# Low parts of the first two batches on GpSimd, another room for VectorE, and an emitted order from the third unit

## The chip, the cores and the metric

The kernel runs on one core of one Trainium2 chip. The metric is device time in microseconds. Three timed runs gave 714.94, 715.07 and 715.30 us; the median is 715.07.

## The reference, cut to what matters

Attention over 4 batches, 8 heads, 576 positions and 64 dimensions a head, and behind it a layer of two products with a squared ReLU:

```python
scores = scale * np.matmul(q, k.transpose(0, 1, 3, 2))
psi_rel = np.log1p(np.abs(rel)); psi_i = np.log1p(np.maximum(pos[:, None], 1.0))
h = np.maximum((psi_rel / psi_i)[..., None] @ w1 + b1, 0.0)
scores = scores + (h @ w2).transpose(2, 0, 1)[None]
attn = np.exp(scores - np.max(scores, axis=-1, keepdims=True))
attn = attn / (np.sum(attn, axis=-1, keepdims=True) + 1e-09)
x = np.matmul(attn, v).transpose(0, 2, 1, 3).reshape(B * S, H * D)
r = np.maximum(x @ w_in, 0.0)
out = (r * r) @ w_out
```

## The kernel before, in words

The attention is cut into 80 units, each of one batch, one pair of heads and one block of query rows. Units 0 to 39 are batches 0 and 1, taken block by block so that the bias, which all batches share, can be made on the way; the first eight are the short last block. Units 40 to 79 are batches 2 and 3, taken pair of heads by pair of heads; every fifth one is a short last block.

In a unit TensorE makes the scores (`sp`), VectorE adds the bias and takes the row extremum (the custom operation on `t`, with `negm`), ScalarE takes the exponential (`p`), TensorE transposes `p` (`pp`, and `pa` for the last columns), ScalarE copies the transposes out (`pt`), and TensorE multiplies with `v` (`px`). In a short last block GpSimd copies 64 columns of `p` first. The tile of scores exists once, so the scores of a unit wait until VectorE has taken the unit before.

The bias is made in 72 steps: VectorE compares distances with thresholds (`mask`), TensorE multiplies the mask with the weights (`bb`), ScalarE and VectorE scale the two results (`bt`), and GpSimd adds them into the table `area`. There are three mask buffers. In units 0 to 7 two or three steps belong to a unit.

The order on an engine comes from two places. Units 0 to 7 run with `plain=True`: a scheduler places their instructions. From unit 8 on the order of TensorE, VectorE and ScalarE is that in which the code emits them, and each bias step first emits the next mask and then its own sum.

In units 40 to 79 the second layer is prepared on the side: weights are read, rounded and split into a high and a low half, and for batches 0 and 1 seven tiles `m` of sums or parts of `x` are made, scaled by `xsig` and split likewise. Five of the seven (`m` = 1, 3, 4, 6, 7) are sums of two blocks; `m` = 2 and 5 are single blocks. Each preparation is a job, a list of stages with an engine, a cost and a function. At the end of every unit `fill` starts the stages whose time has come, as long as the unit's room for that engine lasts; a stage on another engine comes at the earliest a unit later. Before, a sum is three stages: GpSimd adds (`sums_x`), ScalarE scales and rounds to half precision (`high_x`), VectorE scales, subtracts and rounds (`low_x`). Two places hold the sums, so a third sum waits until the first has been used. GpSimd has no room of its own and is not limited.

Behind unit 79 the remaining jobs run out, the first products of the second layer (`ha`, `hb`) begin beside them, and from there TensorE does the second layer: products, a sum of products (`c`), square, split (`gh`, `gl`) and the products with `w_out` (`y`).

Of the kernel before, what the change touches and what calls it, by code (L numbers as in the profile page):

```python
# [17 lines left out]
ALU = mybir.AluOpType  # L18
# [4 lines left out]
HP = H // 2  # L23
# [4 lines left out]
AB = 2  # L28
# [49 lines left out]
def attention_then_relu2_mlp(ctx: ExitStack, tc: tile.TileContext, q, k, v, cols, w_in, w_out, psi, xmat, dist, out):  # L78
    nc = tc.nc
    PE, DVE, ACT, POOL, SP = nc.tensor, nc.vector, nc.scalar, nc.gpsimd, nc.sync  # L80
# [64 lines left out]
    NA = len(units)  # L145
# [352 lines left out]
    def scale_x(b, hp, rows_t):  # L498
        times_rows(b, hp, *spread_rows(rows_t))
# [163 lines left out]
    wdst, xsig, alpha_t = {}, {}, {}  # L663
# [72 lines left out]
    def low_in(n, which=(0, 1)):  # L736
# [5 lines left out]
    width = [256] * B + [128]  # L742
    RIGHT = {
        2: ((0, 0), None, None), 5: ((1, 1), None, None), 3: ((0, 1), ALU.subtract, (1, 1)), 4: ((1, 0), ALU.subtract, (0, 0)),
        1: ((0, 0), ALU.add, (1, 1)), 6: ((0, 0), ALU.add, (0, 1)), 7: ((1, 0), ALU.add, (1, 1)),
    }
    ORDER = (2, 3, 4, 5, 1, 6, 7)
    xs_t = {}
# [15 lines left out]
    split_to = [{m: operand(t[:, 512 * (m - 1):512 * m]) for m in range(1, 8)} for t in xs_at]  # L764
# [7 lines left out]
    def sum_of(n, m):  # L772
        return sum_at.get((n, m), sum_at.get(m))

    def sums_x(n, ms):
        for m in ms:
            for cs, op, a, b in halves(n, m):
                if op:
                    POOL.tensor_tensor(out=sum_of(n, m)[:, :, cs], in0=a, in1=b, op=op)

    def high_x(n, ms):
        for m in ms:
            hi = split_to[n % 2][m][0]
            for cs, op, a, b in halves(n, m):
                ACT.activation(out=hi[:, :, cs], in_=sum_of(n, m)[:, :, cs] if op else a, func=AF.Identity, scale=xsig[n])

    def low_x(n, ms):
        w = width[n]
        for m in ms:
            hi, lo = split_to[n % 2][m]  # L790
            for cs, op, a, b in halves(n, m):
                DVE.scalar_tensor_tensor(out=lo[:, :, cs], in0=sum_of(n, m)[:, :, cs] if op else a, scalar=xsig[n], in1=hi[:, :, cs], op0=ALU.mult, op1=ALU.subtract)
            xs_t[n, m] = (hi[:, :, :w], lo[:, :, :w])

    def store_x(n):
        xs_dram[n] = dram.tile([128, 7 * 512], F32, name=f"xs{n}")
        SP.dma_start(out=xs_dram[n], in_=xs_at[n % 2])
# [40 lines left out]
    def step(s, plain=True):  # L838
        loads(s)
        if plain:  # L840
            scores(s)
        else:
            negm, sps = score_products(s, False)
            exps = [reduce(s, n, negm, sp) for n, sp in enumerate(sps)]
        if s and rest:
            tc.keep_in_program_order(rest.pop(0)())
        n, r = divmod(s, AB * HP)

        def turned():
            for dst, src in transposes((s - TL,)):  # L850
                ACT.copy(dst, src)  # L851

        if not plain:
            rows_made(s - TL)
            turned()
            inverted(s - 1)
            if s >= AB * HP * TAIL:
                scan_first(s)
        if n < TAIL:
            if r == 7 and n + 2 < NIC:  # L860
                tc.keep_in_program_order(scale_xc(chunks[n + 2]))
            if plain:
                bias_upto(NJB * n + BO[r])
                if s == AB * HP - 1:
                    mask_upto(done + MB)
            else:

                def then():
                    mask_upto(done + MB + 1)
                    if exps:  # L870
                        exps.pop(0)()

                sum_upto(NJB * n + BO[r], then)
            if r == 1 and n + 2 < NIC:
                load_xc(chunks[n + 2])
        if plain:
            if s >= TL:
                turned()
        else:
            for fn in exps:  # L880
                fn()
        u = s - TL - 1
        if u >= 0:
            for piece in values((u,)):
                keep_values(*piece)
            if u in norm_of:
                b, hp, ic = units[u]
                scale_x(b, hp, norm_of.pop(u))
# [11 lines left out]
        if u in norm_of:  # L900
            norm_of[u] = norm_copy(norm_rows(norm_of[u]))

    for s in range(AB * HP):
        step(s)
    with tc.manual_schedule(engines={PE.engine, DVE.engine, ACT.engine}):
        for s in range(AB * HP, NA):
            step(s, False)

    scan_stack.close()
# [10 lines left out]
    room = {}  # L920
# [95 lines left out]
    def x_scaled(n, ps_col):  # L1016
        scale_of(n, ps_col)
        if n == 0:
            place_x = raw_tile("w2")
            free = [place_x[:, 512 * k:512 * k + 512] for k in range(2)]  # L1020
            for k, ms in enumerate(((3, 1, 7), (4, 6), (2, 5))):
                stages = []
                for m in ms:
                    if RIGHT[m][1]:
                        sum_at[m] = free[k].rearrange("p (c t) -> p c t", c=2)
                        stages.append(("POOL", 1.3, lambda m=m: sums_x(0, (m,))))
                    stages.append(("ACT", 0.71, lambda m=m: high_x(0, (m,))))
                    stages.append(("DVE", 0.74, lambda m=m: low_x(0, (m,))))
                jobs.insert(len(norms), [max(now[0], first[groups[AB * HP + AB]] + 1), stages])
        else:  # L1030
            free = [a.rearrange("p (c t) -> p c t", c=2) for a in (take(1, 4480, 512), take(0, 9856, 512))]
            for k, ms in enumerate(((3, 1, 7), (4, 6), (2, 5))):
                stages = []
                for m in ms:
                    if RIGHT[m][1]:
                        sum_at[n, m] = free[k]
                        stages.append(("POOL", 1.3, lambda m=m: sums_x(n, (m,))))
                    stages.append(("ACT", 0.71, lambda m=m: high_x(n, (m,))))
                    stages.append(("DVE", 0.74, lambda m=m: low_x(n, (m,))))
                job(dest_at[-1] + 1, *stages)  # L1040

    dest_at = [50] + [60] * 6 + [70]
# [49 lines left out]
    sum_at = {}  # L1092
    with tc.manual_schedule():
        job(NA + 1, *(("DVE", 0.68, lambda k=k: scan(k)) for k in range(SCANS, NF)))
        x_job(NA + 4, 0)
        x_job(NA + 7, 1)
        for u in range(NA - TL - 1, NA):
            norm_job(u)
        for s in range(NA, NU + TL + 3):
            now[0] = s  # L1100
            full = s < NU and units[s][2] < TAIL
            room["DVE"] = min(room.get("DVE", 0), 0.3) + (1.65 if full else 2.5)
            room["ACT"] = min(room.get("ACT", 0) + (0.55 if full else 1.9), 0.6 if full else 1.5)
            loads(s)
            if s == NA:
                for tag, name in zip("dbac", ("pa", "pp", "pp", "px")):
                    held[tag] = bank(name, tag)
                for m, tag in enumerate(raws[:NF - SCANS]):
                    fetch_in(ins[SCANS + m], tag)
            if s < NU:  # L1110
                negm, sps = score_products(s, False)
            fill(s, 3)
            px_now[0] = None
            us = [u for u in ((s - 3, s - 2) if s % 2 else (s - 2, s - 1)) if u < NU]
            pieces = []
            sms = [lambda n=n: softmax(s, n, negm, sps[n]) for n in range(len(sps))] if s < NU else []
            if s % 2 == 0:
                if s == NA and NA - 3 in pt_t:
                    for piece in values((NA - 3,), "c"):
                        keep_values(*piece)  # L1120
                for m, c in enumerate(transposes(us, iter("bacb" if s == NA else "abca")) if us else ()):
                    ACT.copy(*c)  # L1122
            else:
                pieces = values(us, "d") if us else []
            fill(s, 0)
            for fn in sms:
                fn()
            if s < NU and ends(s):
                norm_job(s)
            kept = 0  # L1130
            if any(j[0] <= s and j[1][0][0] == "LAST" for j in jobs):
                kept = max(room["DVE"] - 0.6, 0)
                room["DVE"] -= kept
            fill(s, 1)
            fill(s, 2)
            for piece in pieces:
                keep_values(*piece)
            if kept:
                room["DVE"] += kept
                fill(s, 1)  # L1140
# [31 lines left out]
    sum_at = {3: xT[0][:, 0:2, 128:384], 4: xT[0][:, 2:4, 128:384], 1: take(0, 9856, 512).rearrange("p (c t) -> p c t", c=2)}  # L1172
# [121 lines left out]
    with tc.manual_schedule():  # L1294
# [3 lines left out]
        for i in range(NI + 1):  # L1298
# [4 lines left out]
            n, P = items[min(i, NI - 1)]  # L1303
# [102 lines left out]
```

## Time and profile before

| | |
|---|---|
| median of three runs | 715.07 us |
| profiled execution | 715.1 us |
| its span, first to last instruction | 713.3 us |
| TensorE busy | 685.8 us, 96% |
| VectorE busy | 552.0 us, 77% |
| ScalarE busy | 474.6 us, 67% |
| GpSimd busy | 196.3 us, 28% |
| granted TensorE clock, mean | 0.992 |

The busy share is a mean over stages. Here 1165 instructions of VectorE lie mostly in the first half of the span, in which the attention runs; the second layer leaves VectorE room. A wait of TensorE in the first half moves all that comes behind it.

### The profile page before, as it was taken

To read this page: it belongs to the slowest core of one execution; us is meant where nothing else is said; L and a number is where in the kernel's file an instruction comes from. 1 tells how busy PE (TensorE), PEld (TensorE's weight loads), DVE (VectorE), ACT (ScalarE), POOL (GpSimd) and SP (SyncE) were. 2 spreads that over 40 slices of the span, in tenths; PEclk is the share of its full clock that TensorE was granted. 3 is DMA by queue.
4 is the path that set the end of the run, shared out by engine and by line. 5 is a ranking of instruction groups with operands and counts; after the bars stand their busy time and mean duration, and the time that the engine had idled before them with its cause. 6 is when DMAs were issued, how large, how long until landed. Compare 5 with 4: busy or idle time off the path is not lost.

```text
span 713.3 us, 17398 instructions
## 1 busy us (share of the span) xinstructions
PE 685.8 (96%) x6966; PEld 566.9 (79%) x6966; DVE 552.0 (77%) x1165; ACT 474.6 (67%) x954; POOL 196.3 (28%) x313
## 2 busy tenths in 40 slices
PE   7899999999999999999999999999999999999992
PEld 6568888887787877778788888888888888888881
DVE  8998888876788998998888868687567974566761
ACT  5678878878777999997666757765575554464220
POOL 6564544442111344653223113121111220000000
PEclk9999999999999999999999999999999999999996
DMA  6740000007476134101901433230076403433100
GB/s 190 195 131 3 19 2 3 2 12 230 168 243 208 55 88 131 67 31 51 364 1 61 174 137 119 78 144 1 1 251 250 148 19 145 174 107 119 60 2 29
DMA packets 31620, 75.13 MB, mean 105 GB/s; under 512 B 5556, under 2 KB 13876, under 8 KB 30516
## 3 DMA queue, kind: packets, MB, share of 16 engines
q1 hardware_dynamic: 31540, 74.03, 30.8%
q8 instruction: 55, 0.90, 0.5%
q14 instruction: 25, 0.20, 0.1%
HBM read 55.66 MB, written 18.35 MB: 104 GB/s over the span
## 4 chain that ended last, share of the span: by engine, by line
PE 84%; DVE 8%; ACT 3%; issue 2%; POOL 1%; DMA 0%; SPq 0%; ACTq 0%; DVEq 0%; POOLq 0%
PE y L1283 28%; PE ha L1191 13%; PE px L547 10%; PE sp L425 10%; PE hb L1191 9%; PE pp L529 8%; PE bb L383 4%; DVE t L438 2%; DVE mask L373 2%; ACT pt L1122 1%; PE pa L521 1%; DVE bt L391 1%; ACT p L445 1%; DVE xT L496 0%; PE ra L490 0%
## 5 line engine op out<-in xcount | busy, mean ns | idle before, releaser
L1191 PEld LDWEIGHTS <-area 128*128 128x128 f16 x1680 | 147.7, 98 | 25.3 <-issue 8.7
L1283 PE MATMUL y<-w,gh 128*128 128x512 f32 x576 | 149.0, 398 | 0.6 <-ACT gh L1227 0.6
L1283 PEld LDWEIGHTS y<-w,gh 128*128 128x128 f32 x576 | 105.1, 188 | 22.3 <-ACT gh L1227 1.3
L438 DVE CUSTOM_DVE_ANT_0 t<-sp,area 128x576 f32<-128x576 f32 x144 | 104.2, 754 | 23.0 <-PE sp L425 12.4
L445 ACT ACTIVATE p<-t,negm 128x576 f32<-128x576 f32 x144 | 113.3, 798 | 2.6 <-DVE negm L438 2.0
L425 PE MATMUL sp<-k,q 64*128 64x288 f32 (+1 forms) x640 | 98.8, 426 | 3.3 <-DVE negm L438 1.7
L547 PE MATMUL px<-pt,v 128*64 128x128 f32 (+1 forms) x1600 | 92.2, 266 | 0.9 <-DVE bt L391 0.7
L547 PEld LDWEIGHTS px<-pt,v 128*64 128x64 f32 x1600 | 79.2, 137 | 13.5 <-ACT pt L1122 6.4
L1191 PE MATMUL ha<-area 128*128 128x256 f16 (+1 forms) x816 | 85.1, 260 | 0.7 <-DVE c L1208 0.7
L399 POOL TENSOR_TENSOR area<-bt,bt 128x256 f32<-128x256 f32 x72 | 64.8, 907 | 66.1 <-DVE bt L391 65.9
L1283 PE MATMUL y<-w,gl 128*128 128x512 f32 x288 | 79.0, 390 | 0.0
L529 PE MATMUL pp<-ident,p 128*128 128x128 f32 x576 | 77.6, 277 | 0.9 <-DVE bt L391 0.8
L529 PEld LDWEIGHTS pp<-ident,p 128*128 128x128 f32 x576 | 62.4, 141 | 15.5 <-ACT p L445 6.6
L425 PEld LDWEIGHTS sp<-k,q 64*128 64x128 f32 (+1 forms) x640 | 52.8, 175 | 23.5 <-issue 6.5
L1191 PE MATMUL hb<-area 128*128 128x256 f16 (+1 forms) x612 | 64.7, 260 | 0.0
L1283 PEld LDWEIGHTS y<-w,gl 128*128 128x128 f32 x288 | 54.1, 188 | 12.2 <-DVE gl L1228 0.2
L373 DVE TENSOR_TENSOR mask<-sdist,theta 128x1024 f16<-128x1024 f16 x81 | 58.1, 727 | 2.8 <-PE bb L383 0.6
L851 ACT COPY pt<-pp 128x512 f32<-128x512 f32 x68 | 36.9, 589 | 25.4 <-PE pp L529 25.4
L383 PE MATMUL bb<-wmov,mask 128*128 128x64 f16 x1296 | 46.7, 195 | 5.0 <-DVE mask L373 4.8
L383 PEld LDWEIGHTS <-mask 128*128 128x128 f16 x1296 | 43.8, 100 | 9.3 <-DVE mask L373 7.4
L1122 ACT COPY pt<-pp 128x512 f32<-128x512 f32 x76 | 41.5, 605 | 13.3 <-PE pp L529 13.0
L1228 DVE TENSOR_TENSOR gl<-area,gh 128x512 fp32r<-128x512 f32 (+1 forms) x40 | 25.3, 668 | 27.4 <-ACT gh L1227 25.6
(161 smaller groups left out, 993.0 us busy)
## 6 DMA issues: line engine op xcount, KB each, us to landing
raw<-in_w_in SPq DMA_DIRECT2D x32, 512.0 KB, 3.9
r<-in_w_out SPq DMA_DIRECT2D x16, 512.0 KB, 5.1
xs<-area SPq DMA_DIRECT2D x4, 1792.0 KB, 12.7
py<-o SPq DMA_DIRECT2D x12, 512.0 KB, 3.0
o<-py SPq DMA_DIRECT2D x12, 512.0 KB, 4.5
v<-in_v SPq DMA_DIRECT2D x16, 320.0 KB, 4.1
q<-in_q SPq DMA_DIRECT2D x32, 128.0 KB, 3.3
out<-o SPq DMA_DIRECT2D x8, 512.0 KB, 2.9
```

The source lines that it names most:

```text
L373: DVE.tensor_tensor(out=out, in0=win, in1=th, op=ALU.is_ge)
L383: PE.matmul(bb[:, 64 * (7 - r):64 * (8 - r)], lhsT=m[:, r], rhs=wmov[:, n], start=(n == 0), stop=(n == 1))
L399: POOL.tensor_tensor(out=dst, in0=tw, in1=sw, op=ALU.add)
L425: mm = PE.matmul(out_t[to, x, :HALF], lhsT=qt[rows, cols], rhs=kt[rows, k0:k0 + HALF], start=True, stop=True)
L438: DVE.tensor_tensor_reduce(out=t.rearrange("p (x n) -> p x n", x=2), in0=sp[:, :, :HALF], in1=bias.rearrange("p (x n) -> p x n", x=2), sca ...
L445: ACT.activation(out=p[:, S * n:S * n + S], in_=t, func=AF.Exp, bias=negm[:, n:n + 1], scale=-1.0, accum_out=sums[:, 2 * ic + n:2 * ic + n ...
L529: PE.transpose(pp[:, 128 * c:128 * c + 128], p[:, k0:k0 + 128], ident)
L547: PE.matmul(px[64 * h:64 * h + 64, 128 * m:128 * m + w], lhsT=vt[:, c, h], rhs=src, start=(c == 0), stop=(c == 4))
L851: ACT.copy(dst, src)
L1122: ACT.copy(*c)
L1191: PE.matmul(h[:, s, :w], lhsT=a, rhs=x, start=(k == 0), stop=(k == 5))
L1283: PE.matmul(y_t[n][k], lhsT=(gl if m == 2 else gh)[:, slot, o:o + 128], rhs=wl if m == 1 else wh, start=((n, P) in firsts and f == 0 and m ...
```

## The change

There are three edits. First, units from 2 on, not from 8 on, use the emitted order (`FREE = 2`). Second, for batches 0 and 1 the five sums have other stages: GpSimd adds and multiplies by the scale in place, ScalarE copies the result to half precision, GpSimd subtracts; the two single blocks keep their stages. Third, VectorE's room for a full unit is 1.6 in even and 1.35 in odd units instead of 1.65, and GpSimd gets a room of 3.2 a unit.

```diff
+    def scaled_sum(n, m):
+        sums_x(n, (m,))
+        t = sum_of(n, m)[:, :, :width[n]]
+        POOL.tensor_scalar(out=t, in0=t, scalar1=xsig[n], scalar2=None, op0=ALU.mult)
+
+    def high_sum(n, m):
+        w = width[n]
+        ACT.copy(split_to[n % 2][m][0][:, :, :w], sum_of(n, m)[:, :, :w])
+
+    def low_sum(n, m):
+        w = width[n]
+        hi, lo = (x[:, :, :w] for x in split_to[n % 2][m])
+        POOL.tensor_tensor(out=lo, in0=sum_of(n, m)[:, :, :w], in1=hi, op=ALU.subtract)
+        xs_t[n, m] = (hi, lo)
+
+    def split_stages(n, m, free):
+        if not RIGHT[m][1]:
+            return [("ACT", 0.71, lambda: high_x(n, (m,))), ("DVE", 0.74, lambda: low_x(n, (m,)))]
+        sum_at[n, m] = free
+        return [("POOL", 2.5, lambda: scaled_sum(n, m)), ("ACT", 0.62, lambda: high_sum(n, m)), ("POOL", 1.3, lambda: low_sum(n, m))]
...
-                if s == AB * HP - 1:
+                if s == FREE - 1:
                     mask_upto(done + MB)
...
-    for s in range(AB * HP):
+    FREE = 2
+    for s in range(FREE):
         step(s)
     with tc.manual_schedule(engines={PE.engine, DVE.engine, ACT.engine}):
-        for s in range(AB * HP, NA):
+        for s in range(FREE, NA):
             step(s, False)
...
-                    if RIGHT[m][1]:
-                        sum_at[n, m] = free[k]
-                        stages.append(("POOL", 1.3, lambda m=m: sums_x(n, (m,))))
-                    stages.append(("ACT", 0.71, lambda m=m: high_x(n, (m,))))
-                    stages.append(("DVE", 0.74, lambda m=m: low_x(n, (m,))))
+                    stages += split_stages(n, m, free[k] if k < 2 else None)
...
-            room["DVE"] = min(room.get("DVE", 0), 0.3) + (1.65 if full else 2.5)
+            room["DVE"] = min(room.get("DVE", 0), 0.3) + ((1.6, 1.35)[s % 2] if full else 2.5)
+            room["POOL"] = min(room.get("POOL", 0), 0) + 3.2
```

On VectorE, in units 6 and 7 (`L438` is the bias and extremum of a unit's scores, `L373` a mask, `L391` the scaled result of a bias step), there stood before:

```order
L438 ISA t,negm<-sp,area 128x576
L438 ISA negm 128x1
L373 TENSOR_TENSOR mask<-sdist,theta 128x1024 x3
L391 TENSOR_TENSOR bt_1027<-bb,xc 128x256
L391 TENSOR_TENSOR bt_1051<-bb,xc 128x256
L391 TENSOR_TENSOR bt_1075<-bb,xc 128x256
L438 ISA t,negm<-sp,area 128x576
```

and now there stands:

```order
L438 ISA t,negm<-sp,area 128x576
L438 ISA negm 128x1
L373 TENSOR_TENSOR mask<-sdist,theta 128x1024
L391 TENSOR_TENSOR bt_1039<-bb,xc 128x256
L373 TENSOR_TENSOR mask<-sdist,theta 128x1024
L391 TENSOR_TENSOR bt_1065<-bb,xc 128x256
L373 TENSOR_TENSOR mask<-sdist,theta 128x1024
L391 TENSOR_TENSOR bt_1089<-bb,xc 128x256
L438 ISA t,negm<-sp,area 128x576
```

The instructions are the same; masks and results of bias steps now alternate.

On GpSimd, around units 55 to 59 of the second attention stage (`L779` adds two blocks, `L720` to `L722` are the sums of a weight tile, `L447` the copy of a short block's `p`), there stood before:

```order
L467 CAST parts<-sums 128x9
L779 TENSOR_TENSOR raw<-xT_82 128x512
L720 TENSOR_TENSOR raw<-wa 128x256
L721 TENSOR_TENSOR raw<-wa 128x256
L722 TENSOR_TENSOR raw<-wa 128x128
L779 TENSOR_TENSOR raw<-xT_82 128x512
L447 COPY p<-p 128x64
```

and now there stands (`L798` is the multiplication, `L807` the subtraction, `L734` the high part of a weight tile):

```order
L467 CAST parts<-sums 128x9
L807 TENSOR_TENSOR area<-raw,area 128x512
L779 TENSOR_TENSOR raw<-xT_82 128x512
L798 TENSOR_SCALAR raw<-raw,small 128x512
L720 TENSOR_TENSOR raw<-wa 128x256
L721 TENSOR_TENSOR raw<-wa 128x256
L722 TENSOR_TENSOR raw<-wa 128x128
L807 TENSOR_TENSOR area<-raw,area 128x512
L734 TENSOR_SCALAR area<-wa,small 128x256
L807 TENSOR_TENSOR area<-raw,area 128x512
L779 TENSOR_TENSOR raw<-xT_82 128x512
L798 TENSOR_SCALAR raw<-raw,small 128x512
L447 COPY p<-p 128x64
```

Between the same two copies of small tiles and of `p`, GpSimd has six more instructions: two multiplications, three subtractions and the high part that stood later.

On VectorE, in unit 57 (`L792` is a low part, `L200` and `L201` the last steps of a weight tile, `L197` and `L198` its first steps), there stood before:

```order
L438 ISA t,negm<-sp,area 128x576
L438 ISA negm 128x1
L792 SCALAR_TENSOR_TENSOR area<-raw,small,area 128x512
L200 SCALAR_TENSOR_TENSOR wa<-raw,wa 128x512
L201 SCALAR_TENSOR_TENSOR wa<-raw,wa 128x512
L560 COPY xT_3936<-px 128x64
L560 COPY xT_3937<-px 128x128
```

and now there stands:

```order
L438 ISA t,negm<-sp,area 128x576
L438 ISA negm 128x1
L197 TENSOR_SCALAR wa<-wa 128x512
L198 TENSOR_SCALAR wa<-wa 128x512
L560 COPY xT_3936<-px 128x64
L560 COPY xT_3937<-px 128x128
```

The low part has left VectorE, and the weight tile is two steps further back.

## Rows read from the trace of the kernel before

**Rows 1.** Busy time by engine in 20 us (count), granted clock, DMA share, GB/s:

```profile
240.00:260.00 20.00, 19.49 (x222) 15.38 (x224) 19.40 (x48) 18.80 (x46) 10.74 (x17) 1.00 0.21 58
```

**Rows 2.** Waits of TensorE, 0 to 62 us: total, times, longest:

```profile
PE bb L383 <- DVE mask L373: 4.8, 9, 0.9
```

**Rows 3.** Waits of TensorE, 189 to 326 us:

```profile
PE sp L425 <- DVE negm L438: 1.7, 6, 0.4
PE sp L425 <- DVE sums L459: 1.2, 2, 0.6
```

**Rows 4.** Waits of TensorE, 326 to 700 us:

```profile
PE ha L1191 <- DVE c L1208: 0.7, 1, 0.7
PE y L1283 <- ACT gh L1227: 0.6, 1, 0.6
```

**Rows 5.** Busy time of the masks alone, by stretch, with their count:

```profile
24.00:54.00 30.00, 14.77 (x20) 1.00 0.55 152
54.00:100.00 46.00, 15.34 (x23) 1.00 0.03 9
```

**Rows 6.** Timeline of VectorE, 38 to 58 us (start, length, idle before):

```profile
39.00 0.76 DVE L438 CUSTOM_DVE_ANT_0 t<-sp,area 128x576 f32<-128x576 f32 x1 [0.47 <-PE sp L425]
...
57.52 0.76 DVE L438 CUSTOM_DVE_ANT_0 t<-sp,area 128x576 f32<-128x576 f32 x1 [0.96 <-PE sp L425]
```

**Rows 7.** VectorE by form, 230 to 330 us: busy us, mean ns, idle before:

```profile
L201 DVE SCALAR_TENSOR_TENSOR wa<-raw,wa 128x512 uint32<-128x512 uint32 x7 | 4.8, 692 | 0.2
...
L792 DVE SCALAR_TENSOR_TENSOR area<-area,small 128x512 f16<-128x512 f32 x5 | 4.3, 865 | 0.0
...
L792 DVE SCALAR_TENSOR_TENSOR area<-raw,small,area 128x512 f16<-128x512 f32 x5 | 4.1, 818 | 0.0
```

**Rows 8.** GpSimd by form, 190 to 342 us:

```profile
L467 POOL CAST parts<-sums 128x9 bf16<-128x9 f32 x33 | 8.5, 258 | 26.0 <-DVE sums L460 12.8 <-DVE sums L459 11.8
L734 POOL TENSOR_SCALAR area<-wa,small 128x256 f16<-128x256 f32 x8 | 7.9, 988 | 0.0
...
L779 POOL TENSOR_TENSOR raw<-xT 128x512 f32<-128x512 f32 x5 | 6.5, 1306 | 0.8 <-DVE area L792 0.6 <-DMA v<-in_v 0.2
L721 POOL TENSOR_TENSOR raw<-wa 128x256 f32<-128x256 f32 x8 | 6.5, 808 | 0.0
L469 POOL TENSOR_TENSOR sums<-sums,parts 128x9 f32<-128x9 f32 x22 | 6.3, 288 | 1.8
L720 POOL TENSOR_TENSOR raw<-wa 128x256 f32<-128x256 f32 x8 | 6.2, 780 | 16.8 <-ACT p L445 12.7 <-DVE wa L201 4.1
L722 POOL TENSOR_TENSOR raw<-wa 128x128 f32<-128x128 f32 x8 | 4.8, 602 | 0.0
```

**Rows 9.** Timeline of GpSimd at units 54 and 74:

```profile
245.11 0.24 POOL L447 COPY p<-p 128x64 f32<-128x64 f32 x1 [11.55 <-ACT p L445]
...
313.12 0.24 POOL L447 COPY p<-p 128x64 f32<-128x64 f32 x1 [2.31 <-ACT p L445]
```

**Rows 10.** Timeline of ScalarE at units 60 and 77:

```profile
260.61 0.71 ACT L785 ACTIVATE area<-raw,small 128x512 f16<-128x512 f32 x1
262.26 1.57 ACT L1122 COPY pt<-pp 128x512 f32<-128x512 f32 x3 [0.94 <-PE pp L529]
263.70 0.47 ACT L1122 COPY pt<-pa 128x128 f32<-128x128 f32 x2
...
322.12 0.73 ACT L785 ACTIVATE area<-area,small 128x512 f16<-128x512 f32 x1
```

**Rows 11.** Timeline of TensorE, 250 to 266 us, the values of unit 61:

```profile
265.04 1.20 PE L547 MATMUL px<-pt,v 128*64 128x128 f32 x18
```

**Rows 12.** Timeline of VectorE ahead of the second layer:

```profile
333.33 1.79 DVE L201 SCALAR_TENSOR_TENSOR wa<-raw,wa 128x512 uint32<-128x512 uint32 x1
```

**Rows 13.** Timeline of VectorE, one form beside small and large GpSimd operations:

```profile
250.64 0.43 DVE L198 TENSOR_SCALAR wa<-wa 128x512 int32<-128x512 int32 x1
...
257.73 1.39 DVE L198 TENSOR_SCALAR wa<-wa 128x512 int32<-128x512 int32 x1
```

More of the change, by code (lines that the diff above doesn't have):

```diff
@@ L1023, in x_scaled @@
                 for m in ms:
-                    if RIGHT[m][1]:
[L1025 to L1028, printed above, removed]
+                    stages += split_stages(0, m, free[k].rearrange("p (c t) -> p c t", c=2) if k < 2 else None)
                 jobs.insert(len(norms), [max(now[0], first[groups[AB * HP + AB]] + 1), stages])
@@ L1034, in x_scaled @@
                 for m in ms:
-                    if RIGHT[m][1]:
-                        sum_at[n, m] = free[k]
-                        stages.append(("POOL", 1.3, lambda m=m: sums_x(n, (m,))))
-                    stages.append(("ACT", 0.71, lambda m=m: high_x(n, (m,))))
-                    stages.append(("DVE", 0.74, lambda m=m: low_x(n, (m,))))
+                    stages += split_stages(n, m, free[k] if k < 2 else None)
                 job(dest_at[-1] + 1, *stages)
```

## The prediction

> **What bounds the kernel now.** I read the busy times by stretch first, then the waits of TensorE, and then, for the two stages that the change touches, the timelines of VectorE, GpSimd and ScalarE. TensorE is busy almost throughout, and its clock is granted in full in every stretch quoted here, so time can be won only where TensorE waits. In the second attention stage it is busy 19.49 of 20 us beside a VectorE at 19.40 and a ScalarE at 18.80, while GpSimd, at 10.74, has near half its time free [rows 1]. In the first 62 us the largest wait of TensorE is for masks that VectorE makes, 4.8 us in nine waits [rows 2]. From 189 to 326 us it waits 1.7 and 1.2 us for VectorE, in eight waits before score groups [rows 3]. From 326 to 700 us two waits are left, 0.7 and 0.6 us, both where the second layer begins [rows 4]. After that TensorE runs through to the end, and what is won or lost before is carried to the end in full. The profiled execution took 715.1 us (span 713.3 and 1.8 outside it), the median of the three timed runs is 715.07: the sum below is made against 715.1 and needs no correction.
>
> **The change part by part.**
>
> *Emitted order from unit 2.* No instruction is added or removed. Units 2 to 7 stand on VectorE as mask, sum, mask, sum instead of two or three masks and then the sums, and the value product of a unit comes one unit earlier on TensorE. This is how units from 8 on already stand, and there the rows show what it does to a mask: 23 of them take 15.34 us, 0.67 each, where the 20 before 54 us take 14.77, 0.74 each [rows 5]. The difference is 0.07 x 20 = 1.4 us of VectorE, which bounds TensorE here. The long ones are masks that come second or third in a row, while GpSimd adds up the sums of the bias step before. VectorE's own waits in the stretch, such as the 0.47 us before 39.00, could go too; about 1.1 us are idle there. So the bounds are 2.5 us won and, if an emitted unit makes VectorE wait for its scores as the one at 57.52 does for 0.96 us [rows 6], 0.5 lost. I take 1.4 won, the mask term alone.
>
> The Trainium skill, SBUF — State Buffer, section "SBUF: two separate sides", says that VectorE and GpSimd share one pair of ports as an exclusive lock: an operation in a two-port mode or with two SBUF inputs holds off a GpSimd operation that started later, and is held off by one that started earlier, for the whole instruction. The masks agree with it (0.67 against 0.74). It would make the first stage's term what I took, and it speaks against the next part.
>
> *The low parts.* Ten low passes leave VectorE: five at 865 ns and five at 818 ns, 8.4 us together [rows 7]. In exchange the room that the planner gives VectorE falls from 1.65 to 1.6 and 1.35 a unit, so its list gets shorter in some units and stays as long in others. In unit 57 a low pass and the two last steps of a weight tile become two first steps of another, which are shorter; in units 59 and 60 the list stays about as it was. Of the 2.9 us of waits I let 1.0 go; the bounds are 0 and 2.9.
>
> GpSimd gets ten multiplications and ten subtractions. The subtraction has the shape of the sum, 1.31 us. The multiplication is not in the trace; nearest is the one of half the width, 0.99 us [rows 8]. If its length did not matter it would stay 0.99, if all of it grew 1.98. The two-input operation grows from 0.78 to 1.31 over the same step, a factor 1.68, which would make it 1.66. But at half width the multiplication takes longer than the two-input operation although it reads half as much, so a good part of it is a fixed cost; I take 1.3, the middle of 0.99 and 1.66, and keep 0.99 and 1.98 as ends.
>
> The Trainium skill, GPSIMD Engine Reference, section 4.1 "Engine selection", calls one-input operations there "roughly line-rate"; at its 1.2 GHz that would be 0.43 us for 512 columns. Rows 8 do not agree: 256 columns take 0.99.
>
> What matters is who waits. ScalarE's conversion of a sum now stands behind GpSimd's multiplication, and in ScalarE's queue the copies that empty TensorE's transposes stand behind that conversion. For batch 0 GpSimd cannot begin before its copy at 245.11 is done, at 245.35 [rows 9]. From there to the last multiplication it has seven two-input operations (9.17), the parts of one inverse (3 x 0.258 + 2 x 0.288 = 1.35), the sums of a weight tile (0.78 + 0.81 + 0.60 = 2.19), its high part (0.99), and three multiplications (3.9): 17.6 us, end at 262.95. ScalarE reaches that place at 260.61 and begins the copies behind it at 262.26 [rows 10]. Now they begin 0.52 after 262.95, at 263.47, 1.21 late; they ended at 264.17 and were needed by the values at 265.04 [rows 11], so 0.87 is spare: 0.3 us lost. For batch 1 it begins at 313.36 [rows 9] and has four two-input operations, one inverse and two multiplications before the place that ScalarE reaches at 322.12 [rows 10]: 5.24 + 1.35 + 2.6, end at 322.55, 0.4 lost, no spare counted. Together 0.7 lost; with 0.99 for the multiplication nothing, with 1.98 it is 2.4 + 1.8 = 4.2. On ScalarE itself a conversion replaces an activation of the same width: nothing.
>
> *The end of the stage.* GpSimd's low part of the output tile 2 comes one unit earlier. Before, it fell on a VectorE operation that then took 1.79 us, where that form has a mean of 0.69 [rows 7, 12], just ahead of the sums that TensorE waits for (0.7). I take 0.4 of the 1.3 us [rows 4] as won; bounds 1.3 won and 0.7 lost, if the later weight tile comes late from GpSimd.
>
> Sum: -1.4 - 1.0 + 0.7 - 0.4 = -2.1, so 713.0 us.
>
> **The rivals.**
>
> *GpSimd becomes the bound.* The place is unit 59 and unit 77, where ScalarE waits for the multiplication with all its copies behind it. For it: the queue above is full without a gap for 17.6 us, VectorE has some sixteen operations of the locking kind beside it, and one such operation was held 1.39 us instead of 0.43 by a sum of GpSimd [rows 13]. Against it: only half of GpSimd is used now. With 1.98 for the multiplication 4.2 us are lost; if two of the sixteen are held as that one was, 1.9 us, VectorE's gain of 1.0 turns into a loss of 0.9; the end gives nothing. -1.4 + 0.9 + 4.2 = +3.7: 718.8 us. It decides when GpSimd's waits and locks cost more than 4.2 us, 1.4 above the 2.8 that the other parts bring.
>
> *The parts cancel.* With 1.66 for the multiplication GpSimd costs 1.4 + 1.15 = 2.6, the masks give 1.4, VectorE 1.0 and the end nothing: +0.2, 715.3 us. The same comes out if the emitted order does not do what it says, because the scores wait as at 57.52, and the rest stays as forecast less the end: about 714.8.
>
> *GpSimd is never late.* If the multiplication stays under one us, its term is nothing, more of VectorE's waits go (2.2), the masks give 1.8 and the end 1.0: -5.0, 710.1 us. Against it stands the 0.99 at half width.
>
> **How the numbers follow.** The forecast, 711.5 to 713.6, gets 0.42, GpSimd never late 0.10, the parts cancel 0.30, GpSimd the bound (with all between 716.5 and 720) 0.18. A measurement here tells 0.2%, 1.4 us, from no change; so faster 0.52, same 0.30, slower 0.18. The range runs from 710.8, in the case without lateness, to 716.9, part of the way to the slow rival, and leaves about one in ten on each side.
>
> **What would show it.** Unit 10's first score group before 58.4 instead of 59.66, with masks before 54 us at 0.67 to 0.69 on the mean, shows the first term. The multiplication's mean says which case holds: above 1.6 the forecast fails. ScalarE's conversions waiting for GpSimd, in units 57, 59 and 77, show the loss; TensorE's waits for VectorE from 189 to 326 us should fall from 2.9 to about 1.9. The forecast is wrong if TensorE waits for copies or values behind those conversions for more than 3 us in sum, or if VectorE's forms beside GpSimd grow so that its busy time does not fall by at least 5 us.

## The result and the profile after

The changed kernel takes 722.29 us (median of four runs, 722.02 to 722.63) against 715.11 us: ratio 1.0102, interval 1.009 to 1.0114. Of all runs below, one of e1 and one of the kernel before took 1146.87 and 947.99 us at a granted clock of 0.56 and 0.68; they are left out of the ratios. The forecast was 713.0 with a range up to 716.9. It was slower by 7.2 us where a gain of 2.1 was forecast. The rival in which GpSimd becomes the bound had the direction and the places, and gave 718.8.

Where the time went is read from the beginning of units on TensorE (the first score product of each, in the traces of both kernels):

| first score product of | before, us | after, us | after minus before |
|---|---|---|---|
| unit 10 | 59.66 | 58.56 | -1.10 |
| unit 58 | 253.05 | 252.01 | -1.04 |
| unit 59 | 256.64 | 257.16 | +0.52 |
| unit 61 | 263.87 | 264.98 | +1.11 |
| unit 62 | 266.86 | 269.39 | +2.53 |
| unit 72 | 300.48 | 303.08 | +2.60 |
| unit 73 | 304.28 | 307.94 | +3.66 |
| unit 78 | 321.09 | 325.25 | +4.16 |
| unit 79 | 324.39 | 330.15 | +5.76 |
| second layer (`y`) | 342.94 | 350.05 | +7.11 |

So 1.1 us are won in the first stage, 3.6 lost in units 58 to 61, 1.06 in unit 72, 0.5 in 75 to 77, 1.6 in unit 78 and 1.35 ahead of the second layer. (The start of the second layer is that of its first product with `w_out`, `y`.) After that both kernels run alike.

What TensorE waits for from 189 to 333 us in the changed kernel, and then ahead of the second layer (total, times, longest; [rows 3, 4] are those of before):

```profile
PE pp L529 <- ACT rows L479: 3.0, 2, 1.6
PE sp L425 <- DVE negm L438: 2.3, 6, 0.5
PE pa L521 <- POOL p L447: 1.0, 1, 1.0
PE sp L425 <- DVE sums L459: 0.9, 2, 0.6
PE pa L521 <- DVE xT L560: 0.8, 1, 0.8
PE px L547 <- ACT pt L1137: 0.8, 1, 0.8
...
PE ha L1206 <- DVE c L1223: 1.5, 1, 1.5
PE y L1298 <- ACT gh L1242: 0.7, 1, 0.7
PE hb L1206 <- DVE c L1225: 0.3, 1, 0.3
```

The waits for VectorE before score groups were 2.9 and are 3.2: nothing has gone there. New are the waits for ScalarE's rows and copies, for GpSimd's copy of a `p` and for VectorE's `xT`. Behind the first of them stands ScalarE, and behind ScalarE GpSimd. What ScalarE waits for from GpSimd, 240 to 330 us (total, times, longest):

```profile
ACT area L802 <- POOL raw L798: 5.4, 2, 3.4
ACT area L802 <- POOL area L798: 1.9, 1, 1.9
```

GpSimd in the same stage, by form (busy us, mean ns; [rows 8] are those of before):

```profile
L798 POOL TENSOR_SCALAR area<-area,small 128x512 f32<-128x512 f32 x5 | 8.8, 1769 | 0.5
...
L798 POOL TENSOR_SCALAR raw<-raw,small 128x512 f32<-128x512 f32 x5 | 8.4, 1678 | 1.5 <-DVE small L225 1.1
...
L807 POOL TENSOR_TENSOR area<-raw,area 128x512 f16<-128x512 f32 x5 | 5.8, 1164 | 0.0
```

The multiplication takes 1.68 and 1.77 us on the mean, 1.57 where nothing disturbs it; 1.3 had been taken, with 1.98 as the upper end. The subtraction takes 1.16, less than the 1.31 of a sum. The queue of batch 0 in time order, to be read beside [rows 9] (start, length, and in brackets the idle time before with its releaser):

```profile
235.28 1.57 POOL L798 TENSOR_SCALAR raw<-raw,small 128x512 f32<-128x512 f32 x1
243.69 0.24 POOL L447 COPY p<-p 128x64 f32<-128x64 f32 x1 [6.84 <-ACT p L445]
243.89 1.17 POOL L807 TENSOR_TENSOR area<-raw,area 128x512 f16<-128x512 f32 x1
...
253.43 1.62 POOL L798 TENSOR_SCALAR raw<-raw,small 128x512 f32<-128x512 f32 x1
...
262.42 2.06 POOL L798 TENSOR_SCALAR raw<-raw,small 128x512 f32<-128x512 f32 x1
264.43 0.23 POOL L447 COPY p<-p 128x64 f32<-128x64 f32 x1
```

Three things stand here. GpSimd is idle for 6.84 us because the first subtraction is queued behind the copy of a `p` that has to wait for a softmax; ScalarE had the high part ready at 240.0. Then the queue is full: from 243.89 to the end of the last multiplication at 264.48 it runs 20.6 us without a gap. And the next copy of a `p`, at 264.43, is itself behind that multiplication, so TensorE waits directly for GpSimd. ScalarE and TensorE at the two places:

```profile
255.08 0.62 ACT L802 CAST area<-raw 128x512 f16<-128x512 f32 x1 [2.06 <-POOL raw L798]
...
264.51 0.62 ACT L802 CAST area<-raw 128x512 f16<-128x512 f32 x1 [3.37 <-POOL raw L798]
```

```profile
255.92 0.66 PE L529 MATMUL pp<-ident,p 128*128 128x128 f32 x4 [1.62 <-ACT rows L479]
...
264.72 0.33 PE L521 MATMUL pa<-ident,p 128*128 128x128 f32 x1 [1.04 <-POOL p L447]
...
266.98 1.89 PE L547 MATMUL px<-pt,v 128*64 128x128 f32 x40 [0.76 <-ACT pt L1137]
```

VectorE was to have 8.4 us less to do. Its busy time over the whole stage, from the first score product of unit 40 to 6 us past that of unit 79, before and after (second number after the window: TensorE, then weight loads, VectorE, ScalarE, GpSimd, each with its count):

```profile
189.74:330.39 140.65, 137.42 (x1615) 110.40 (x1612) 123.39 (x313) 123.71 (x304) 49.99 (x106) 1.00 0.37 116
```

```profile
188.64:336.15 147.51, 138.44 (x1615) 110.57 (x1612) 121.60 (x306) 122.20 (x304) 79.29 (x126) 1.00 0.36 111
```

VectorE fell by 1.8 us only, while GpSimd rose by 29.3. Three steps of weight tiles came into this stretch from behind it, but that is the smaller part: from unit 40 to the first `y`, VectorE's 333 and 323 instructions differ by the ten low passes and nothing else, and its busy time is 134.2 us before and 133.4 after. So nearly all of the 8.4 went back into operations that became longer. In unit 72, VectorE's list now has two pairs of first steps of a weight tile in a row, beside the sums of a weight tile and of batch 1 on GpSimd:

```profile
302.84 0.55 DVE L197 TENSOR_SCALAR wa<-wa 128x512 f32<-128x512 f32 x1
303.42 0.83 DVE L198 TENSOR_SCALAR wa<-wa 128x512 int32<-128x512 int32 x1
304.18 0.68 DVE L197 TENSOR_SCALAR wa<-wa 128x512 f32<-128x512 f32 x1
304.89 1.38 DVE L198 TENSOR_SCALAR wa<-wa 128x512 int32<-128x512 int32 x1
```

Two pairs are 1.7 us alone (0.42 and 0.43 each); here they are 3.4, and unit 73 begins 1.06 us later.

### The profile page after: what moved, and what is told of

Same layout as the page of the kernel before. It is cut to its first block, busy times and chain, and to the rows that moved or that the text cites. A ratio compares the mean times of both kernels' runs of the same rounds, so it can differ in the third digit from the quotient of the medians.

```text
span 720.3 us, 17411 instructions
## 1 busy us (share of the span) xinstructions
PE 685.8 (95%) x6966; PEld 567.5 (79%) x6966; DVE 551.3 (77%) x1155; ACT 471.9 (66%) x954; POOL 225.9 (31%) x333
## 4 chain that ended last, share of the span: by engine, by line
PE 83%; DVE 6%; POOL 4%; ACT 2%; issue 2%; DMA 1%; SPq 0%; ACTq 0%; POOLq 0%; DVEq 0%
PE y L1298 28%; PE ha L1206 13%; PE sp L425 10%; PE px L547 9%; PE hb L1206 9%; PE pp L529 8%; PE bb L383 4%; DVE mask L373 1%; DVE t L438 1%; ACT pt L1137 1%; POOL area L807 1%; PE pa L521 1%; POOL raw L798 1%; POOL raw L779 1%; DMA raw<-in_w_in 1%
## 5 line engine op out<-in xcount | busy, mean ns | idle before, releaser
L438 DVE CUSTOM_DVE_ANT_0 t<-sp,area 128x576 f32<-128x576 f32 x144 | 104.2, 753 | 28.4 <-ACT p L445 13.1
L373 DVE TENSOR_TENSOR mask<-sdist,theta 128x1024 f16<-128x1024 f16 x81 | 58.0, 720 | 2.5 <-PE bb L383 0.5
L720 POOL TENSOR_TENSOR raw<-wa 128x256 f32<-128x256 f32 x16 | 12.2, 763 | 111.9 <-issue 65.8
```

What stands on the lines that cost most here:

```text
L373: DVE.tensor_tensor(out=out, in0=win, in1=th, op=ALU.is_ge)
L438: DVE.tensor_tensor_reduce(out=t.rearrange("p (x n) -> p x n", x=2), in0=sp[:, :, :HALF], in1=bias.rearrange("p (x n) -> p x n", x=2), sca ...
```

## The experiments

Four theories stood against each other. Theory 1: GpSimd's own work is too long, and ScalarE waits for its multiplications. Theory 2: two-input operations of GpSimd and VectorE's operations hold each other. Theory 3: the low parts stand in GpSimd's queue behind the copy of a `p`. Theory 4: the rooms place VectorE's list badly. Times below are medians of a kernel's runs, ratios are against the kernel before on the same chip. Profiled executions of the same first stage differ by up to 1.3 us there (unit 10 begins at 57.94 in e11 and at 59.28 in e5; the last section tells of the clock behind it), so single places are compared by the length of units.

**e1: the emitted order alone** (`FREE = 2` on the kernel before).

> The kernel before with the emitted order from unit 2 and nothing else. All theories that put the loss behind 240 us say that the 1.1 us won at unit 10 in the changed kernel stay to the end: 714.0. If the gain of the first stage was given back later (a wait that only moved), 715.1.

713.74 us, ratio 0.9984 (0.9975 to 0.9994). The first part of the change is a gain of 1.1 us that stays to the end. All that follows is compared with this kernel; the changed one is 8.6 us above it (8.4 by the ratios, since the two were timed on different chips).

**e2: no multiplication.**

```diff
     def scaled_sum(n, m):
         sums_x(n, (m,))
-        t = sum_of(n, m)[:, :, :width[n]]
-        POOL.tensor_scalar(out=t, in0=t, scalar1=xsig[n], scalar2=None, op0=ALU.mult)
```

> The changed kernel without the ten multiplications on GpSimd; the sums of batches 0 and 1 stay unscaled, so their values are others. Theory 1 (GpSimd's own work is too long, ten times 1.7 us, and ScalarE waits for it): the waits of ScalarE for GpSimd of 2.1, 3.4 and 1.9 us go, and of the 8.3 us lost behind unit 10 at least 5 come back: 716 to 717.5. Theory 2 (GpSimd's two-input operations and VectorE hold each other; a multiplication reads one operand and does not count): 721 to 722. Theory 3 (the first low parts stand in GpSimd's queue behind the copy of a p and start 3.7 us late, the length of the work is secondary): 719 to 720.

718.26 us, ratio 1.005 (1.0037 to 1.0063): 4.0 us come back, less than theory 1 said and more than theories 2 and 3. ScalarE no longer waits for GpSimd at all, yet 4.5 us of the 8.6 are left. One loss has even grown: units 54 to 57 take 1.7 us longer than before, where the changed kernel had 0.4, and TensorE waits 5.2 us for VectorE before score groups. Where GpSimd is not late, its operations meet VectorE's at another place.

**e3: the copy of `p` on ScalarE** (second attention stage only).

```diff
-                POOL.tensor_copy(out=p[:, S:S + 64], in_=p[:, S - 64:S])
+                (ACT.copy if u >= NA else POOL.tensor_copy)(p[:, S:S + 64], p[:, S - 64:S])
```

> The changed kernel with the copy of a short block's p, in the second attention stage, on ScalarE in place of GpSimd; nothing in GpSimd's queue waits for a softmax any more. Theory 3: the first low part starts at 240.0 instead of 243.9, the wait of TensorE for the p copy (1.0) goes too, and 3 to 4 us of batch 0's 3.7 come back, nothing of batch 1's: 718.3 to 719.3. Theory 1: GpSimd is full from 244 to 264 all the same and ScalarE only waits a little less: 721 to 722. Theory 2: 722.

719.48 us, ratio 1.007 (1.0057 to 1.0083): 2.8 us come back with no instruction less. The first subtraction now begins when ScalarE has its high part:

```profile
239.69 1.17 POOL L807 TENSOR_TENSOR area<-raw,area 128x512 f16<-128x512 f32 x1 [3.24 <-ACT area L802]
```

and ScalarE's waits for GpSimd fall from 7.3 to 0.3 us. Theory 3 explains the larger part of batch 0's loss: units 54 to 61 are 1.7 us longer than before instead of 4.0. Units 72 to 78 are 3.3 us longer, in the changed kernel 3.2, although ScalarE's wait of 1.9 there is gone. What remains in this kernel is VectorE's: TensorE waits 6.3 us for it before score groups (2.9 before), the longest 1.7.

**e4: the rooms of before** (VectorE 1.65, no limit for GpSimd).

> The changed kernel with VectorE's room at 1.65 again and no limit on GpSimd's: the planner lets GpSimd begin its work sooner. Theory 4 (the room tables place the work badly): 719 to 720.5. Theories 1 and 2: within 1 us of the changed kernel, 721.3 to 723.3, since no work goes.

725.12 us, ratio 1.0147 (1.0134 to 1.0161). A miss on both sides: ScalarE's waits for the multiplications grow from 7.3 to 10.1 us, and in the profiled execution TensorE's granted clock falls to 0.50 from 252 to 254 us (1.2 GHz, the lower of its two levels), behind four us in which TensorE was busy 2.0. The two new rooms together are not what makes the changed kernel slow. What each of them is worth this run does not show, since it sets back both, and in that execution a part of the 2.8 us is the clock's.

**e5: emitted order and copy of `p` on ScalarE, low parts on VectorE.**

> The kernel before with the emitted order from unit 2 and the copy of p on ScalarE, the low parts still on VectorE. The copy mattered only where GpSimd is full: then nothing is gained beside the emitted order alone, 713.7 (713.3 to 714.1). If the copy by itself helps or hurts (ScalarE gets eight copies of some 0.2 us), 712.7 or 714.7.

714.62 us, ratio 0.9999 (0.999 to 1.0008). Without the low parts on GpSimd the copy gains nothing; it costs some 0.9 us against e1, so the 2.8 of e3 are the queue's. The cost arises by unit 58: GpSimd begins a sum at 243.29 now, no longer behind the copy, and beside its sums VectorE's `L201` at 243.85 takes 1.65 us and its `L198` at 250.87 takes 1.38, where e1 has 0.69 and 0.43. That is theory 2 in a kernel that has no low part on GpSimd.

**e6: a one-input operation in place of the subtraction** (with the copy as in e3).

```diff
-        POOL.tensor_tensor(out=lo, in0=sum_of(n, m)[:, :, :w], in1=hi, op=ALU.subtract)
+        POOL.tensor_scalar(out=lo, in0=hi, scalar1=ones[:, 0:1], scalar2=None, op0=ALU.mult)
```

> The changed kernel with the copy of p on ScalarE, and in place of GpSimd's subtraction (two operands from memory) a multiplication by one of the high part (one operand, same width, same place in the queue); the low parts then hold the high parts. What is left over of the loss beside the copy alone (719.5 against 713.7) is 5.8 us. Theory 2 (locks by two-input operations): ten of twenty two-input operations of GpSimd go, so VectorE's operations of the forms L197, L198, L200, L201 and L792 are held less, and 2 to 4 us come back: 715.5 to 717.5. Theory 1 (length of GpSimd's work): the replacement is no shorter (1.2 to 1.7 instead of 1.16), so 719.5 to 721.

718.58 us, ratio 1.0053 (1.004 to 1.0066), 0.9 under e3: between the two. The replacement took 1.62 us instead of 1.16, so it was no clean test: fewer full holds, but longer work. That one-input operations lengthen VectorE's too is shown by the table under e9.

**e7: copy on ScalarE and no multiplication.**

> The changed kernel with the copy of p on ScalarE and without the ten multiplications (values unscaled). Either alone gave 718.3 (no multiplications) and 719.5 (copy). Theory 2: with ScalarE no longer waiting for GpSimd, the rest is locks by sums and subtractions, which neither edit touches: 717.8 to 718.6, the two don't add up. If the length of GpSimd's work still matters after the waits of ScalarE are gone, they add up: 715.5 to 716.5.

717.75 us, ratio 1.0037 (1.0024 to 1.005). The edits do not add up: both take away ScalarE's wait for GpSimd, which is 0.3 us in e3 already. Still the multiplications' going gives 1.7 us against e3, so they cost by another way too (table under e9). What is left, 4.0 us above e1, is not ScalarE's wait.

**e8 and e10: one batch only.** In e8 batch 1's low parts are on VectorE again, in e10 batch 0's (there with VectorE's room at 1.65).

> The changed kernel with the low parts of batch 1 on VectorE again (batch 0's stay on GpSimd), the rooms as in the changed kernel. Of the 8.6 us between the emitted order alone and the changed kernel, 3.6 arose by unit 62, the rest from unit 72 on: if the two batches are separate stretches, 713.7 + 3.6 = 717.3, with the later part as in the emitted order alone; if batch 1's loss comes from what batch 0's left behind (a planner's backlog, the smaller rooms), 720 to 722.

> The changed kernel with the low parts of batch 0 on VectorE and VectorE's room at 1.65 again; batch 1's stay on GpSimd, GpSimd's room 3.2. Batch 0 alone gave 719.4, 5.7 above the emitted order; both give 8.6. If the batches add up, batch 1 costs 2.9: 716.6. If the queue of GpSimd is short enough with one batch, 714 to 715.

e8: 719.42 us, ratio 1.0064 (1.005 to 1.0079). e10: 717.38 us, ratio 1.0033 (1.0021 to 1.0046). Above e1 that is 5.7 and 3.6, together 9.3 against the 8.6 of the full change: the batches about add up, though the two runs have different rooms. e10 was missed by 0.8 and e8 by 2.1: the 1.06 of unit 72 is in e8 as well, though batch 1 is on VectorE, and it is not in e10. So it hangs on the rooms and not on the low parts.

**e9: no low parts at all** (the ten are set to zero by a memset of 0.53 us on GpSimd; copy of `p` on ScalarE, rooms as changed).

> The changed kernel with the copy of p on ScalarE and no low parts of the ten sums at all: no multiplication, no subtraction, only a memset of the low parts to zero on GpSimd (the values lack the low parts); ScalarE scales as before the change. Planner, rooms and VectorE's list stay as changed. Theory 2 (what is left beside the copy and the multiplication, 717.75 against 713.74, comes of VectorE and GpSimd holding each other): most of the 4.0 goes, 713.5 to 715; the 1.06 at unit 72 stays, since it is sums of a weight tile and of batch 1 that hold VectorE there and they stay. Theory 4 (VectorE's list under the new rooms is late by itself): 717 to 718.

716.05 us, ratio 1.0016 (1.0007 to 1.0025). Of the 5.7 us between e3 and e1, 3.4 hang on what GpSimd does for the low parts. VectorE shows it. From unit 40 to the second layer, e3 and e9 have the same list of VectorE's instructions in the same order. In the stage of the attention they take (the first is e3, VectorE third)

```profile
188.30:333.50 145.20, 137.73 (x1615) 110.66 (x1612) 124.02 (x306) 124.61 (x312) 76.69 (x118) 1.00 0.35 113
```

```profile
188.94:330.20 141.26, 137.64 (x1615) 110.43 (x1612) 118.19 (x306) 124.64 (x312) 51.25 (x108) 1.00 0.36 116
```

so 5.8 us of VectorE's time are there because of what GpSimd does beside it. e6 and e7 have this list too:

| all with the copy on ScalarE | GpSimd's work for the low parts | VectorE busy, 306 instructions, us | time, us |
|---|---|---|---|
| e3 | ten multiplications, ten subtractions | 124.0 | 719.48 |
| e6 | ten multiplications, ten multiplications by one | 122.9 | 718.58 |
| e7 | ten subtractions | 120.5 | 717.75 |
| e9 | ten memsets | 118.2 | 716.05 |

Theory 2 had said that a multiplication, which reads one operand, does not count. It does: the ten of them are 3.5 us of VectorE's time between e3 and e7, the ten subtractions 2.3 between e7 and e9.

But 2.3 us of the loss against e1 stay in e9 although nobody makes low parts any more, and neither theory had that: 1.05 at unit 72, and 1.4 from unit 79 to the second layer, where three waits are 2.4 us together (1.3 in two waits in e1):

```profile
PE ha L1204 <- DVE c L1221: 1.4, 1, 1.4
PE y L1296 <- ACT gh L1240: 0.7, 1, 0.7
PE hb L1204 <- DVE c L1223: 0.3, 1, 0.3
```

**e11: VectorE's room 1.75 and 1.55 by parity, on e1.**

> The emitted order from unit 2 with the low parts on VectorE and its room at 1.75 in even and 1.55 in odd units, in place of 1.65. A candidate: of the 2.9 us of waits for VectorE between 189 and 326 us, 1 may go (712.7) if they come of odd units with too long a list; if the lists are late wherever they stand, 713.2 to 714.7.

713.68 us, ratio 0.9983 (0.9974 to 0.9992): the same as e1. The two are the fastest kernels found; both beat the kernel before and the changed one.

**e12: one tile of ten** (the first of batch 0 on GpSimd, VectorE's room 1.65; GpSimd's room of 3.2 stays, which e1 does not have).

> The emitted order from unit 2, VectorE's room 1.65, and only one of the ten low parts (the first tile of batch 0, where GpSimd stands idle for 7 us) on GpSimd, its multiplication 1.57 and subtraction 1.17. A candidate: VectorE's list is 0.84 shorter in one unit: 713.0 to 713.7 if nothing is held; 714 to 715 if the planner only fills the room with a step that GpSimd holds.

716.29 us, ratio 1.0012 (1.0003 to 1.0021); above both expected ranges. Its runs fall into two groups, near 714.5 at a mean granted clock of 0.993 and near 716.6 at 0.989, with one between. VectorE, then GpSimd, in the profiled execution, which is of the slower group:

```profile
248.61 1.72 DVE L792 SCALAR_TENSOR_TENSOR area<-xT,small,area 128x512 f16<-128x512 f32 x1
250.26 1.50 DVE L197 TENSOR_SCALAR wa<-wa 128x512 f32<-128x512 f32 x1
251.79 0.58 DVE L198 TENSOR_SCALAR wa<-wa 128x512 int32<-128x512 int32 x1
```

```profile
248.63 1.15 POOL L807 TENSOR_TENSOR area<-raw,area 128x512 f16<-128x512 f32 x1
249.87 1.60 POOL L779 TENSOR_TENSOR raw<-xT 128x512 f32<-128x512 f32 x1
```

The low pass of 0.75 is held through the whole subtraction to 250.34, and the next step, 0.42 alone, through the sum to 251.76: 2.05 us, and TensorE's longest wait for scores here is 2.0. This is theory 2 at one place, without any lateness of GpSimd: ScalarE waits for no multiplication in this kernel. The wait has a sequel on TensorE (busy first, granted clock third from the end):

```profile
252.00:254.00 2.00, 0.13 (x2) 0.16 (x4) 2.00 (x6) 0.92 (x3) 0.62 (x1) 1.00 0.00 0
254.00:256.00 2.00, 2.00 (x12) 1.29 (x13) 1.18 (x4) 1.58 (x4) 0.00 (x0) 0.67 0.03 8
256.00:258.00 2.00, 2.00 (x12) 2.00 (x11) 2.00 (x6) 1.17 (x2) 0.27 (x1) 0.50 0.00 0
```

Behind the wait the clock is at the lower of its two levels (1.2 GHz) until about 258, and unit 58 takes 1.33 us longer than in e1. So the 2.6 us against e1 are two things: the faster group is 1.1 above the faster of e1's two groups (near 713.4), and that is the tile's price; in the slower group the clock comes on top. The changed kernel has no such fall in this stage.

**e13, e14 and e15: the remaining 2.3 us.** In e13 and e15 VectorE's room is 0.9 smaller in unit 71 (e13 on e9, e15 on e3), and only VectorE's list changes; e14 is e9 with VectorE's room at 1.65.

> The kernel without the ten low parts of e9, with VectorE's room 0.9 smaller in unit 71 alone: its two pairs of first steps (L197, L198 twice, 3.4 us beside GpSimd's sums) come one unit later, one pair to a unit; no other engine's list changes. If the pairs are the 1.05 at unit 72: 715.0, and unit 73 begins where it does in the emitted order. If they are held the same a unit later: 716.0.

> The kernel without the ten low parts of e9, with VectorE's room at 1.65 in every unit as before the change (GpSimd's room stays). If the smaller rooms place VectorE's list badly: 713 to 714.5, no more than the emitted order alone. If any list that takes the place of the low passes meets GpSimd's sums, 715.5 to 717.

> The changed kernel, low parts on GpSimd, with the copy of p on ScalarE and the two pairs moved as in e13. If the parts of the loss add up: 719.5 less 1.05, 718.4. If GpSimd's fuller queue holds the moved pairs too: 719.0 to 720.

e13: 715.91 us (1.0014, 1.0005 to 1.0023). Unit 72 now is 0.5 us shorter than in e1 instead of 1.05 longer, but units 74 to 77 give the same 1.5 back: the moved steps meet GpSimd there. In VectorE's list of e13 one of them reads

```profile
305.03 2.00 DVE L197 TENSOR_SCALAR wa<-wa 128x512 f32<-128x512 f32 x1
```

against 0.42 alone. e15: 719.36 us (1.0062, 1.005 to 1.0075), the same. e14: 714.46 us (0.9994, 0.9986 to 1.0003): the smaller rooms cost 1.6 us of the 2.3, and ahead of the second layer TensorE waits no more. (The room alone does not settle that place: e10 has 1.65 too, with batch 1's low parts on GpSimd, and `ha` waits 1.5 us there.) But even with ten low passes fewer on VectorE and none on GpSimd, e14 is no faster than e1, which has them. VectorE is busy 126.8 us from unit 40 to the second layer instead of 134.2, and still TensorE's waits before score groups are 4.6 us, where before had 2.9. The copy of `p` is not what hides a gain here: its cost in e5 arose by unit 58, and up to there e14 has lost nothing against e1.

## Why the prediction was wrong

Three of the four terms of the sum failed. The largest is GpSimd's lateness, +0.7, which was 5.2; the low parts on VectorE and the end of the stage had the wrong sign.

- *Emitted order, -1.4.* Right in size, -1.1 (e1), for another reason than the one chosen. The masks are hardly shorter (25 of them take 18.5 us instead of 18.7, 0.75 each instead of 0.77, where 0.07 each had been forecast), so the reason that the prediction read from 0.67 against 0.74 is not borne out. VectorE's idle time is: from the first score product of unit 0 to that of unit 10, before and after, VectorE (third engine) is busy for the same time in a shorter stretch,

```profile
18.07:59.66 41.59, 37.27 (x648) 27.84 (x645) 39.19 (x86) 29.82 (x73) 22.16 (x30) 1.00 0.51 140
```

```profile
17.89:58.56 40.67, 37.31 (x647) 29.64 (x644) 39.14 (x86) 28.87 (x73) 22.53 (x30) 0.96 0.50 144
```

  idle 2.40 before and 1.53 now. That was the other part of this term, named as a bound and not taken. The sign, unit 10 before 58.4, is missed by 0.16; in e13, whose clock stays up in this stage, unit 10 begins at 58.03.
- *Low parts off VectorE, -1.0.* Failed, about +1.5 (units 72 and 75 to 77). The step took ten passes away and left the length of the rest as it was. But what is left meets GpSimd, which has 29 us more to do, and gets longer: the busy time fell by 1.8 instead of at least 5, the bound that the prediction had set itself, and e3 against e9 puts 5.8 us of VectorE on GpSimd's work for the low parts. The smaller rooms were counted as a gain; 1.06 of the 1.5 is unit 72, where they set two pairs of steps in a row (in e9 too, not in e10). And in e14, with the passes gone from both engines, TensorE waits no less before scores: with this planner the gain was not there to be had.
- *Waiting for GpSimd, +0.7.* The mechanism was right, the size wrong: 5.2 us (units 58 to 61 and unit 78). The sum ran 17.6 us from the copy to the last multiplication; it is 20.6. The three multiplications are 5.25 instead of 3.9, the parts of the inverse 2.3 instead of 1.35, the sums of the weight tile 2.8 instead of 2.19; the last two had been priced undisturbed, though VectorE stands beside them. The sum was also made for one place in each batch only. In batch 0 ScalarE reaches an earlier multiplication at 253.0 and waits for it until 255.05, with the rows of an inverse behind it, and on GpSimd the copy of a `p` stands behind the last one. The prediction asked who queues behind ScalarE's conversion, and not who queues behind the multiplication on GpSimd itself.
- *The copy that GpSimd waits for.* [Rows 9] were read as the time at which the queue can begin. They were also the remedy: moving this copy gives 2.8 us back (e3).
- *End of the stage, -0.4.* Failed, +1.35. The low part that comes earlier is no gain, since three steps of the next weight tile take its place just ahead of `c`, beside sums on GpSimd. VectorE in the changed kernel, to be read beside [rows 12]:

```profile
338.97 1.27 DVE L197 TENSOR_SCALAR wa<-wa 128x512 f32<-128x512 f32 x1 [0.56 <-ACT wa L195]
340.28 0.84 DVE L198 TENSOR_SCALAR wa<-wa 128x512 int32<-128x512 int32 x1
341.15 1.10 DVE L200 SCALAR_TENSOR_TENSOR wa<-r,wa 128x512 int32<-128x512 int32 x1
```

  They are 1.54 alone and 3.2 here, and `ha` waits 1.5 instead of 0.7.
- *The rival "GpSimd becomes the bound"*, 718.8, had the right mechanism, near the right price for lateness (4.2 against 5.2) and for holding (+0.9 against +1.5, this one partly by luck, since 1.06 of it hangs on the rooms). It took the end as nothing and was still 3.5 short: 1.0 and 0.6 in these two, 1.35 at the end, 0.3 in the first stage and 0.2 that the parts do not cover. A chance of 0.18 was too little for it: the row with the hold of 0.96 us in [rows 13] was counted for two operations of sixteen. In the changed kernel twelve of the twenty first steps of weight tiles (`L197`, `L198`) from unit 40 to the second layer are longer by more than a quarter, three of them at 1.27 to 1.38 us; before, seven of the twenty were, two of them at 1.38 and 1.39.

The measured parts sum to -1.1 + 5.2 + 1.5 + 1.35 = +7.0; measured are +7.2. Left open is how ScalarE's lateness and the holds divide at each wait, since e2 and e3 move both, and where the lateness goes the holds grow (units 54 to 57, and 75 and 77 in e3); and whether there is an order of VectorE's and GpSimd's lists in which the holds vanish. No run tried that.

## What to carry to other kernels

Moving work to an engine that is half idle is priced by its queue, not by its load: note from when the queue can begin, add every operation up to each place where another engine reaches for its result, and look at what else stands in that queue. Where two engines hold each other, work taken off one and put on the other comes back as longer operations on both, and a planner's smaller room can set what remains in a worse place (unit 72). One tile moved alone (e12) tells that early, if the granted clock is read beside the time.

## What the hardware showed

- A multiplication by a scalar on GpSimd, 512 columns of f32, takes 1.57 us undisturbed, more than a sum of two tiles of the same width (1.27 to 1.31); the subtraction that writes f16 takes 1.16.
- VectorE's operation of 0.42 to 0.75 us is held past the end of a two-input operation of GpSimd (e12: 1.72 and 1.50). Beside a multiplication of GpSimd it is stretched, which sums to 3.5 us for ten multiplications (e3 against e7). This one in the changed kernel, 0.69 alone, lies wholly inside a multiplication that runs from 314.42 to 316.30.

```profile
314.90 1.06 DVE L201 SCALAR_TENSOR_TENSOR wa<-raw,wa 128x512 uint32<-128x512 uint32 x1
```

  Both get longer there (the multiplication 1.88 instead of 1.57). The Trainium skill, SBUF — State Buffer, section "SBUF: two separate sides", has the shared ports as an exclusive lock for the whole instruction; the two-input rows agree with it, and these two operations, which run side by side as far as GpSimd's recorded times go, do not.
- The emitted order makes TensorE wait once for 2.2 us near 27 us, and in some executions its granted clock then falls to the lower of its two levels (1.2 GHz) for some 3 us. e1 and e13, the same first stage (busy time by engine, granted clock third from the end):

```profile
28.00:30.00 2.00, 1.18 (x8) 0.68 (x8) 2.00 (x7) 0.92 (x3) 1.16 (x2) 0.96 0.89 277
30.00:32.00 2.00, 2.00 (x22) 1.83 (x21) 1.90 (x5) 0.74 (x2) 1.48 (x3) 0.50 0.68 169
```

```profile
28.00:30.00 2.00, 1.32 (x9) 0.82 (x10) 2.00 (x6) 0.87 (x2) 1.16 (x2) 1.00 0.88 275
30.00:32.00 2.00, 2.00 (x55) 1.94 (x55) 2.00 (x5) 1.44 (x4) 1.34 (x3) 1.00 0.66 174
```

  In 30 to 32 us TensorE is busy throughout in both, with 22 products in the one and 55 in the other. By unit 10 the difference is 0.53 us, about that between the two groups of e1's runs (near 713.4 and 714.0). In e12 a wait of 1.97 us in the second attention stage has the same sequel, and unit 58 takes 1.33 us longer for it.
